# Splitting a late load, regrouping the norm work and thinning the TensorE fillers ahead of the main loop of a fused attention and feed-forward kernel

## The chip, the cores and the metric

The kernel runs on one core of a Trainium2 chip. The metric is the device time of one execution in microseconds. Engines are called as the profile calls them: PE is TensorE's matmul and PEld its weight load, DVE is VectorE, ACT is ScalarE, POOL is GpSimd and SP is SyncE; the last two mostly issue DMAs here.

## The reference, cut to what matters

Two steps are fused. The first is a cross-covariance attention over channels; the second a two-layer network with a squared ReLU. Shapes are B = 4, N = 6080, C = 256, and 2048 hidden features.

```python
qn = q / (norm(q, axis=1) + 1e-6)          # a norm for each of 256 channels, over 6080 rows
kn = k / (norm(k, axis=1) + 1e-6)
s = kn.transpose(0, 2, 1) @ qn / tau       # 256 x 256 for each batch
a = softmax(s)                             # each row divided by its sum
x = (v @ a).reshape(B * N, C)
h = maximum(x @ w_in, 0)
out = (s_moe * h * h + b_moe) @ w_out
```

## The kernel before

The attention matrix is never applied to v. For each batch the kernel forms the Gram matrix of q and k, turns it into exponentials, and multiplies these by `w_in`, which gives a folded weight `wa` of 256 x 2048. The main loop then takes v in groups of 512 rows: 16 steps of `mm1` (L761, `h_ps`) with `wa`, ReLU and square on ACT and DVE, and the second product (L932, `o_ps`). The norms and Gram matrices of batches 1 to 3 are worked in between the steps of the main loop by a table of steps. The change lies in batch 0 alone, which has to be finished before the first step of the main loop.

Batch 0 goes like this. Its 6080 rows are cut into chunks (`make_chunks`): eleven chunks of 128 partitions x 4 rows, then one of 128 x 2 and one of 96 x 2, thirteen in all, numbered 0 to 12. For each chunk k and q are loaded and cast to half precision by the DMAs of the POOL queue (`Gram.load`, L137); three of the first four loads go in fp32 through the SP and ACT queues and are cast by DVE and ACT (L145). At most eight DMAs of the POOL queue are under way: each later one waits for the landing of the one eight places before.

`Gram.mm` (L154) adds a chunk to the Gram matrix `s_ps`: 2 matmuls of 256 columns for each of its rows. `norm_ops` squares the chunk, k on ACT (L185) and q on DVE (L182) or, in odd chunks, on ACT; it folds the squares of four rows to one on DVE (two adds, L199) and adds that to the sum of chunk 0 (`into_first`, L213, held as `f`).

The last `NLATE` = 3 chunks are late ones: all their k parts are loaded before their q parts, so that k's norms can be done while q is still coming. Their squares are kept apart (`late_pool`), and `add_norms` sums them over the partitions on TensorE: for k with a matrix of ones into 256 columns (L252, one matmul for each row), for q into one column (L256, two for each row). The first late chunk's four k squares are first added to two on DVE (`half`, L229). The order of the end is written out by hand: k's squares and sums; then the chunk sum `f` (`last_sum`, the L213 of chunk 9); the inverse norms of k (`inverse`, L277: four ACT steps, Ln, Exp of a half, Ln, Exp of minus one); then for each late chunk q's squares, its matmuls and its sums, where the last chunk's sums come ahead of its matmuls; then four ACT steps for q's inverse norms, `scale` (L302, two DVE multiplications of `s_ps` by k's inverse norms), the transposes of the first v group (L469), and `first_block`. `first_block` has for each half of the channels an exponential (L308, scaled by q's inverse norm), row sums (L347) and two matmuls of 256 columns into `wa_ps` (L352); then the reciprocal `rs` (L356) and four 128-column evictions to `wa` on ACT (L329) and DVE (L331). The next blocks of `wa` are folded between the first steps of the main loop (L336).

`keep_busy` issues matmuls whose result nobody reads (fillers, L554): 512 columns of FP32R ones. `FILL` names after which chunk, counted from the end, and how many: one after each of chunks 5, 6 and 7, two after each of 8 and 9. One more stands behind the transposes of v.

The queues work in program order, which the kernel fixes with `po(...)` around each instruction.

Of the kernel before, what the change touches and what calls it, by code (L numbers as in the profile page):

```python
# [16 lines left out]
def kernel(  # L17
# [30 lines left out]
    NG = (NT + TG - 1) // TG  # L48
    NP = FT // 2
    SHIFT = 3  # L50
    NLATE = 3
    assert CH == 2 and FT == 16
    v_flat = v.rearrange("b n c -> (b n) c")

    def po(ins):

        tc.keep_in_program_order(ins)
        return ins
# [47 lines left out]
        return chunks  # L106

    whole = N // (P * JC)
    chunks_first = make_chunks([JC] * whole + [2, 2])
    chunks_later = make_chunks([JC] * (whole + 1))  # L110

    class Gram:
# [7 lines left out]
        def load(self, c, parts=(0, 1)):  # L120

            at, np_, jc = self.chunks[c]
            if 0 in parts:
                self.raw[c] = qk_pool.tile([P, 2, JC, C], FP16, tag="qk", name="qk")
            t = self.raw[c]
            for i in parts:
                src = (k, q)[i]
                rows = src[self.b, at : at + np_ * jc, :].rearrange("(p j) c -> p j c", j=jc)
                if self.b == 0 and (c, i) in DIRECT:
                    if c == i == 0:  # L130
                        for h, queue in enumerate((nc.sync, nc.scalar)):
                            ps = ts(h, P // 2)
                            queue.dma_start(out=raw32[ps, 0], in_=rows[ps])
                    else:
                        (nc.sync, nc.scalar)[i].dma_start(out=raw32[:, DIRECT.index((c, i))], in_=rows)
                else:
                    po(nc.gpsimd.dma_start(out=t[:np_, i, :jc, :], in_=rows))  # L137
            self.tiles[c] = t[:, 1], t[:, 0]

        def cast(self, c):  # L140

# [21 lines left out]
        def norm_ops(self, c):  # L163

            qc, kc = self.tiles[c]
            _, np_, jc = self.chunks[c]
            st = {}

            at_end = self.b == 0 and c >= len(self.chunks) - NLATE

            def squares(a, js):
                def f():
                    if "sq" not in st:
                        if at_end:
                            st["sq"] = late_pool.tile([P, 2, jc, C], FP16, tag=f"sq{c}", name="sq")
                        else:
                            st["sq"] = sq_pool.tile([P, 2, JC, C], FP16, tag="sq", name="sq")
                    if a == 1 and at_end and c == len(self.chunks) - 1:
                        po(nc.vector.tensor_mul(
                            st["sq"][:np_, 1, js, :], kc[:np_, js, :], kc[:np_, js, :]))  # L180
                    elif a == 0 and (self.b > 0 or at_end or c % 2 == 0):
                        po(nc.vector.tensor_mul(  # L182
                            st["sq"][:np_, 0, js, :], qc[:np_, js, :], qc[:np_, js, :]))
                    else:
                        po(nc.scalar.activation(  # L185
                            out=st["sq"][:np_, a, js, :], in_=(qc, kc)[a][:np_, js, :],
                            func=AF.Square))
                return f

            def fold(half, arrays, last):  # L190
                def f():
                    src = st["f", 2 * half] if 2 * half < jc else st["sq"]
                    if ("f", half) not in st:
                        if last:
                            t = f3_pool.tile([P, 2, 1, C], FP16, tag="f3", name="f3")
                        else:
                            t = sq_pool.tile([P, 2, half, C], FP16, tag=f"f{half}", name="f")
                        st["f", half] = t
                    po(nc.vector.tensor_add(  # L199
                        st["f", half][:np_, arrays], src[:np_, arrays, :half, :],  # L200
                        src[:np_, arrays, half : 2 * half, :]))
                    if last and c == 0:
                        self.first = st["f", half]
                    if last and c == 0:
                        for rows in self.rows:
                            rows.append((st["f", half], np_, 1))
                return f

            def into_first():

                dst, src = self.first[:np_], st["f", 1][:np_]
                if self.b == 0:
                    po(nc.vector.tensor_add(dst, dst, src))  # L213
                else:
                    po(nc.gpsimd.dma_start(out=dst, in_=src, accum_op=ALU.add))  # L215

            def unfolded(a):
                self.rows[a].append((st["sq"], np_, jc))

            ops = []  # L220
            for h in range(0, jc, 4):
                js = slice(h, min(h + 4, jc))
                ops += [squares(1, js), squares(0, js)]
            if at_end:
                def rows(a):
                    if a == 0 or jc == 2:
                        return unfolded(a)
                    half = sq_pool.tile([P, 2, 2, C], FP16, tag="f2", name="half")
                    po(nc.vector.tensor_add(half[:np_, 1], st["sq"][:np_, 1, :2], st["sq"][:np_, 1, 2:]))  # L229
                    self.rows[1].append((half, np_, 2))  # L230
                return ops + [rows]
            if jc == 8:
                ops += [fold(4, slice(0, 1), False), fold(4, slice(1, 2), False)]
            ops += [fold(2, slice(0, 2), False), fold(1, slice(0, 2), True)]
            return ops + [into_first] if c > 0 else ops
# [24 lines left out]
        def finish_ops(self):  # L260
# [3 lines left out]
            def inverse(a=None):  # L264

                n = C + CH if a is None else (CH, C)[a]

                def part(i):
                    if i == 0:
                        st["r", a] = sm_pool.tile([P, n], FP32, tag=f"r{a}", name=f"r{a}")  # L270
                        if a is None:
# [20 lines left out]
                self.add_norms(1)  # L292
                self.add_norms(0, last=True)

            def scale(halves=1):
                rk, src = st["r", 1], st.get("t", self.s_ps)
                if "t" not in st:
                    st["t"] = sm_pool.tile([P, CH, C], FP32, tag="sm_t", name="sm_t")
                for h in range(halves):
# [40 lines left out]
            def first_block(n):  # L340
# [3 lines left out]
                for j in range(CH):  # L344
# [4 lines left out]
                                            stop=(ch == CH - 1 and j == CH - 1),  # L349
                                            skip_group_check=True))  # L350
                    for m in range(CH):
                        po(nc.tensor.matmul(two[m], st["e"][:, j, ts(m, P)],  # L352
                                            w_in16[:, j, :n],
                                            start=(j == 0), stop=(j == CH - 1)))
                st["rs"] = sm_pool.tile([P, CH], FP32, tag="rs", name="rs")
                po(nc.vector.reciprocal(out=st["rs"], in_=r_ps))  # L356
                for f0 in range(0, n, P):
# [71 lines left out]
            if self.b == 0:  # L429
                blocks = [(2 * P, 2 * P), (4 * P, 2 * P), (6 * P, 2 * P), (2 * NW, NW), (3 * NW, NW)]  # L430
                folds = [fold_one(f0, n, m) for f0, n in blocks for m in range(CH)]
                return [norms(1), *inverse(1), norms(0), *inverse(0), lambda: scale(CH),
                        lambda: first_block(2 * P)] + folds

            def sums_and_halves():
# [75 lines left out]
                out=ident16, in_=ones_id, compare_op=ALU.is_equal, fill=0.0, base=0,  # L511
                pattern=[[-1, P]], channel_multiplier=1))

    for parts in ((0,), (1,)):
        for c in range(len(g0.chunks) - NLATE, len(g0.chunks)):
            g0.load(c, parts)
    NW = 512
    w_in_rows = moe_w_in.rearrange("(co p) f -> p co f", p=P)

# [26 lines left out]
    g0.start()  # L546
    NCH0 = len(g0.chunks)

    FILL = {-8: 1, -7: 1, -6: 1, -5: 2, -4: 2}

    def keep_busy(n):

        for _ in range(n):
            po(nc.tensor.matmul(h_tile("idle_ps")[:, 0, :], fill[:, :P], fill, start=True,  # L554
                                stop=True, skip_group_check=True))

    norms_k, *rest = g0.finish_ops()
    inverse_k, norms_q, inverse_q, scale_s, first_block, folds = (
# [2 lines left out]
    for c in range(NCH0 - NLATE):  # L561
        ops = g0.norm_ops(c)
        for j in range(g0.chunks[c][2]):
            g0.mm(c, j)
        keep_busy(FILL.get(c - NCH0, 0))
        if c == NCH0 - NLATE - 1:
            ops, last_sum = ops[:-1], ops[-1]
        for f in ops:
# [26 lines left out]
    keep_busy(1)  # L595
# [47 lines left out]
    def w_in_sums(i):  # L643
# [1 line left out]
        F = Dff // 2  # L645
        B = lambda k, n: w_in16[:, k, ds(n * F, F)]
        if not W:
            c0, c1, c2 = range(NCH0 - NLATE, NCH0)
            W["T1"] = late_pool.tile([P, F], FP16, tag=f"sq{c1}", name="T1w")
            W["T2"] = late_pool.tile([P, F], FP16, tag=f"sq{c2}", name="T2w")  # L650
            both = late_pool.tile([P, 2, F], FP16, tag=f"sq{c0}", name="TNw")
            W["T3"], W["N4"] = both[:, 0], both[:, 1]
# [376 lines left out]
```

## Time and profile before

| | us |
|---|---|
| median of 3 runs | 714.32 (714.3 to 714.35) |
| span of the profiled execution | 712.9 |
| time of the profiled execution beside its span | not given by the page |
| first `h_ps` matmul of the main loop (L761) | 37.84 |
| last k transfer on the chain of waits, start and length | 21.00, 9.47 |
| TensorE busy in 38 to 710 us | 671.96 of 672 |

The page counts busy time for each engine, shows the span in 40 slices, and follows the chain of work that ended last. PEclk is the clock granted to TensorE as a share of full speed. Its record begins at 16.8 us here; earlier stretches are printed as 1.00, though the 27 matmuls that start between 11 and 16.5 us take 420 ns on average, and the 20 that start between 17 and 20 us take 276 ns. Times of instructions are counted from the start of the span.

### The profile page before, as it was taken

Reading aid. Unit: us, or ns where it says so; the run is one execution under the profiler, and the core shown is the slowest. Engines: PE = TensorE matmul, PEld = TensorE weight load, DVE = VectorE, ACT = ScalarE, POOL = GpSimd, SP = SyncE. Lnnn points to the kernel's source line nnn. Section 1 sums busy time; section 2 is a strip of 40 time slices with the busy share of each in tenths; the row PEclk is TensorE's granted clock in tenths of the full one; section 3 lists DMA queues with packets and bytes.
Section 4 is the critical chain, followed back from the end, with each engine's and each line's share of the span. In section 5 each row is a group of like instructions: output and inputs, shape, how many; then the busy total and the mean of one; then the engine's idle time right before and its main releaser. Section 6 shows DMA issues by size and latency. Waiting matters only on the chain.

```text
span 712.9 us, 17531 instructions
## 1 busy us (share of the span) xinstructions
PE 692.9 (97%) x7422; PEld 502.9 (71%) x7422; DVE 635.6 (89%) x906; ACT 547.5 (77%) x598; POOL 114.1 (16%) x192
## 2 busy tenths in 40 slices
PE   3699999999999999999999999999999999999998
PEld 2456777776677777777677777777768777777777
DVE  4889999999988989998999899998998888888886
ACT  5689877787777777778877777777876777777875
POOL 4533132201202222111010222111000000000000
PEclk9999999999999999999999999999999999999999
DMA  9999999566566878465761888737323333321202
GB/s 213 207 259 168 186 164 137 114 109 122 105 136 109 133 137 144 110 92 101 156 131 50 148 134 150 129 76 96 101 65 75 94 71 75 97 61 46 83 31 75
DMA packets 87854, 83.55 MB, mean 117 GB/s; under 512 B 56368, under 2 KB 62784, under 8 KB 87776
## 3 DMA queue, kind: packets, MB, share of 16 engines
q0 software_dynamic: 27136, 44.00, 38.9%
q1 hardware_dynamic: 60128, 37.45, 21.1%
q8 instruction: 58, 0.95, 0.6%
q10 hardware_dynamic: 512, 0.98, 0.4%
q14 instruction: 20, 0.16, 0.1%
HBM read 78.91 MB, written 24.90 MB: 146 GB/s over the span
## 4 chain that ended last, share of the span: by engine, by line
PE 95%; DMA 4%; ACT 1%; issue 0%; DVE 0%; ACTq 0%; POOLq 0%
PE h_ps L761 46%; PE o_ps L932 40%; PE s_ps L154 5%; DMA qk<-in_q_dram 2%; DMA qk<-in_k_dram 1%; PE wa_ps L394 1%; PE o_ps L836 1%; PE o_ps L808 0%; PE wa_ps L336 0%; ACT r L277 0%; PE n_ps L252 0%; ACT sq L185 0%; ACT eT L308 0%; PE vT_ps L469 0%; DVE half L229 0%
## 5 line engine op out<-in xcount | busy, mean ns | idle before, releaser
L771 ACT ACTIVATE r<-h_ps 128x1024 f16<-128x1024 f32 (+1 forms) x384 | 388.5, 1013 | 144.2 <-PE h_ps L761 140.6
L761 PE MATMUL h_ps<-vT,wa 128*128 128x512 f16 (+7 forms) x1632 | 452.1, 364 | 0.5 <-ACT wa L329 0.5
L932 PEld LDWEIGHTS <-S 128*128 128x128 f16 x2944 | 198.1, 98 | 84.3
L932 PEld LDWEIGHTS <-g 128*128 128x128 f16 x2208 | 155.0, 98 | 74.0
L784 DVE TENSOR_TENSOR g<-r 128x2048 f16<-128x2048 f16 (+2 forms) x150 | 174.4, 1163 | 10.1 <-ACT r L771 9.7
L932 PE MATMUL o_ps<-T,S 128*128 128x128 f16 x2208 | 183.1, 219 | 0.0
L761 PEld LDWEIGHTS <-wa 128*128 128x128 f16 x1632 | 136.6, 98 | 19.0 <-ACT wa L329 1.0
L932 PE MATMUL o_ps<-w_out,g 128*128 128x128 f16 x1472 | 134.2, 219 | 0.0
L782 ACT ACTIVATE g<-r 128x1024 f16<-128x1024 f16 (+1 forms) x97 | 100.3, 1034 | 0.2
L789 DVE SCALAR_TENSOR_TENSOR o_sb<-o_ps,s_out,u 128x256 f32<-128x256 f32 x138 | 66.2, 480 | 36.1 <-PE o_ps L932 34.5
L154 PE MATMUL s_ps<-qk 128*128 128x256 f16 (+1 forms) x384 | 71.0, 287 | 15.6 <-ACT qk L145 11.0
L458 POOL DMA_DIRECT2D v<-in_v_dram x48 | 31.4, 662 | 239.9 <-DMA vT<-v 192.7
L215 POOL DMA_DIRECT2D f<-f x33 | 28.8, 874 | 245.9 <-DVE f L199 197.3
L789 DVE SCALAR_TENSOR_TENSOR u<-o_ps,s_out,rowconst 128x256 f32<-128x256 f32 x138 | 65.7, 476 | 0.0
L932 PE MATMUL o_ps<-w_out,S 128*128 128x128 f16 x736 | 63.5, 219 | 0.0
L932 PE MATMUL o_ps<-N,g 128*128 128x128 f16 x736 | 63.4, 219 | 0.0
L185 ACT ACTIVATE sq<-qk 128x1024 f16<-128x1024 f16 (+2 forms) x53 | 54.5, 1041 | 4.5 <-DMA qk<-in_k_dram 1.9
L861 DVE TENSOR_TENSOR S<-S,g 128x2048 f16<-128x2048 f16 (+1 forms) x47 | 56.4, 1200 | 1.2
L859 DVE TENSOR_TENSOR S<-g 128x2048 f16<-128x2048 f16 (+1 forms) x47 | 56.0, 1192 | 0.0
L863 DVE TENSOR_TENSOR S<-g 128x2048 f16<-128x2048 f16 x46 | 55.8, 1214 | 0.0
L865 DVE TENSOR_TENSOR S<-g,S 128x2048 f16<-128x2048 f16 x46 | 55.8, 1213 | 0.0
L154 PEld LDWEIGHTS <-qk 128*128 128x128 f16 (+1 forms) x384 | 33.0, 103 | 21.2 <-ACT qk L145 11.0
(103 smaller groups left out, 334.4 us busy)
## 6 DMA issues: line engine op xcount, KB each, us to landing
out_dram<-o_sb SPq DMA_DIRECT2D x43, 512.0 KB, 3.0
v<-in_v_dram POOLq DMA_DIRECT2D x47, 256.0 KB, 5.0
qk<-in_q_dram POOLq DMA_DIRECT2D x43, 256.0 KB, 7.7
qk<-in_k_dram POOLq DMA_DIRECT2D x42, 256.0 KB, 6.4
f<-f POOLq DMA_DIRECT2D x30, 128.0 KB, 3.1
vT<-v SPq DMA_TRANSPOSE x182, 3.0
w<-in_moe_w_out_dram POOLq DMA_DIRECT2D x4, 512.0 KB, 9.9
out_dram<-o_sb SPq DMA_DIRECT2D x8, 256.0 KB, 4.1
```

Of the source, the lines that this page charges most:

```text
L154: po(nc.tensor.matmul(self.s_ps[:, ch, :], qc[:np_, j, ts(ch, P)], kc[:np_, j, :], start=(c == 0 and j == 0 and ch == 0), stop=(c == len(s ...
L185: po(nc.scalar.activation(out=st["sq"][:np_, a, js, :], in_=(qc, kc)[a][:np_, js, :], func=AF.Square))
L761: po(nc.tensor.matmul(dst, wa[:, ci, ts(m, P)], src, start=(ci == 0), stop=(ci == CH - 1), skip_group_check=True))
L771: po(nc.scalar.activation(out=r16[:, :, i % 2, :n], in_=h_tiles.pop((g, i))[:, :, :n], func=AF.Relu))
L782: po(nc.scalar.activation(out=dst, in_=src, func=AF.Square))
L784: po(nc.vector.tensor_mul(dst, src, src))
L789: po(nc.vector.scalar_tensor_tensor(out=dst, in0=src, scalar=s_out, op0=ALU.mult, in1=add, op1=ALU.add))
L859: po(nc.vector.tensor_add(T[1], A21, A22))
L861: po(nc.vector.tensor_sub(T[2], T[1], A11))
L863: po(nc.vector.tensor_sub(T[3], A11, A21))
L865: po(nc.vector.tensor_sub(T[4], A12, T[2]))
L932: po(nc.tensor.matmul(st[name][:, j, :], a()[:, i, ts(j, P)], w[:, i, :], start=first, stop=last, skip_group_check=True))
```

## The change

It does the following.

- Chunks: the eleventh four-row chunk of batch 0 is treated as two chunks of two rows that share one tile. There are now fourteen chunks, of which the last four, 10 to 13, are late ones. Its k part is loaded by one DMA as before, its q part by two (`load_late`).
- q's squares of the last chunk that is not late (chunk 9) are done by DVE, not by ACT.
- The `half` add is left out: all late k squares are summed as they are, nine matmuls in place of seven. `last_sum` is issued ahead of the late k squares.
- The last chunk's q sums come behind its Gram matmuls.
- q's inverse norms: the first two steps stay on ACT; then DVE adds EPS and takes the reciprocal. The first half of `scale` is put ahead of these two, the second behind them.
- `first_block`: for each half of the channels only the first 128 columns are multiplied; the other 128 follow after both.
- Fillers: one after chunk 8 and one after chunk 9, with operands read as FP32 and not FP32R. The one behind the transposes stays.
- The four late square tiles are reused for the four weight sums of the later folds, one tile each.

```diff
-    NLATE = 3
+    NLATE = 4
...
-    chunks_first = make_chunks([JC] * whole + [2, 2])
+    chunks_first = make_chunks([JC] * (whole - 1) + [2] * 4)
+    at_late = chunks_first[-4][0]
...
+        def load_late(self, i):
+            c = len(self.chunks) - NLATE
+            if i == 0:
+                self.raw[c] = qk_pool.tile([P, 2, JC, C], FP16, tag="qk", name="qk")
+                for h in range(2):
+                    t = self.raw[c][:, :, ts(h, 2)]
+                    self.tiles[c + h] = t[:, 1], t[:, 0]
+            rows = (k, q)[i][self.b, ds(at_late, P * JC)].rearrange("(p j) c -> p j c", j=JC)
+            for js in [slice(0, JC)] if i == 0 else [ts(h, 2) for h in range(2)]:
+                po(nc.gpsimd.dma_start(out=self.raw[c][:, i, js], in_=rows[:, js]))
+            for c in range(c + 2, len(self.chunks)):
+                self.load(c, (i,))
...
-                    elif a == 0 and (self.b > 0 or at_end or c % 2 == 0):
+                    elif a == 0 and (self.b > 0 or at_end or c % 2 == 0 or c == len(self.chunks) - NLATE - 1):
...
                 def rows(a):
-                    if a == 0 or jc == 2:
-                        return unfolded(a)
-                    half = sq_pool.tile([P, 2, 2, C], FP16, tag="f2", name="half")
-                    po(nc.vector.tensor_add(half[:np_, 1], st["sq"][:np_, 1, :2], st["sq"][:np_, 1, 2:]))
-                    self.rows[1].append((half, np_, 2))
+                    return unfolded(a)
...
                 def part(i):
+                    if a == 0 and i >= 2:
+                        r = st["r", 0]
+                        if i == 2:
+                            po(nc.vector.tensor_scalar_add(out=r, in0=r, scalar1=EPS))
+                        else:
+                            po(nc.vector.reciprocal(out=r, in_=r))
...
+                        return
...
-                        po(nc.tensor.matmul(two[m], st["e"][:, j, ts(m, P)],
-                                            w_in16[:, j, :n],
-                                            start=(j == 0), stop=(j == CH - 1)))
+                        po(nc.tensor.matmul(two[m][:, :P], st["e"][:, j, ts(m, P)],
+                                            w_in16[:, j, :P], start=(j == 0),
+                                            stop=(j == CH - 1), skip_group_check=True))
+                for m in range(CH):
+                    for j in range(CH):
+                        po(nc.tensor.matmul(two[m][:, P:n], st["e"][:, j, ts(m, P)],
+                                            w_in16[:, j, P:n], start=False,
+                                            stop=(j == CH - 1), skip_group_check=True))
...
-    for parts in ((0,), (1,)):
-        for c in range(len(g0.chunks) - NLATE, len(g0.chunks)):
-            g0.load(c, parts)
+    for i in range(2):
+        g0.load_late(i)
...
-    FILL = {-8: 1, -7: 1, -6: 1, -5: 2, -4: 2}
+    FILL = {-6: 1, -5: 1}
...
-        keep_busy(FILL.get(c - NCH0, 0))
+        keep_busy(FILL.get(c - NCH0, 0), lambda t: t.bitcast(FP32))
...
+    last_sum()
     for c in late:
         k_squares, _, into_rows = ops[c]
         k_squares()
         into_rows(1)
         g0.add_norms(1)
-    last_sum()
...
         ops[c][2](0)
-        if c == NCH0 - 1:
-            norms_q()
         for j in range(g0.chunks[c][2]):
             g0.mm(c, j)
         if c < NCH0 - 1:
             g0.add_norms(0)
-    for f in (*inverse_q, scale_s):
+        else:
+            norms_q()
+    for f in (*inverse_q[:2], lambda: scale_s(0), *inverse_q[2:], lambda: scale_s(1)):
         f()
```

More of the change, by code (lines that the diff above doesn't have):

```diff
@@ L268, in part @@
                 def part(i):
+                    if a == 0 and i >= 2:
[4 more added lines that the diff above has]
+                            po(nc.vector.reciprocal(out=r, in_=r))
+                            if inv_tau != 1.0:
+                                po(nc.vector.tensor_scalar_mul(out=r, in0=r, scalar1=inv_tau))
+                        return
                     if i == 0:
@@ L293, in norms_both, with scale @@
                 self.add_norms(0, last=True)
-            def scale(halves=1):
-                rk, src = st["r", 1], st.get("t", self.s_ps)
+            def scale(halves=1, only=None):
+                rk, src = st["r", 1], st.setdefault("src", st.get("t", self.s_ps))
                 if "t" not in st:
                     st["t"] = sm_pool.tile([P, CH, C], FP32, tag="sm_t", name="sm_t")
-                for h in range(halves):
+                for h in range(halves) if only is None else (only,):
                     js = slice(h, h + 1) if halves == CH else slice(0, CH)
@@ L431, in finish_ops @@
                 folds = [fold_one(f0, n, m) for f0, n in blocks for m in range(CH)]
-                return [norms(1), *inverse(1), norms(0), *inverse(0), lambda: scale(CH),
+                return [norms(1), *inverse(1), norms(0), *inverse(0), lambda h: scale(CH, h),
                         lambda: first_block(2 * P)] + folds
@@ L547, with keep_busy @@
     NCH0 = len(g0.chunks)
-    FILL = {-8: 1, -7: 1, -6: 1, -5: 2, -4: 2}
-    def keep_busy(n):
+    FILL = {-6: 1, -5: 1}
+    def keep_busy(n, cast=lambda t: t):
         for _ in range(n):
-            po(nc.tensor.matmul(h_tile("idle_ps")[:, 0, :], fill[:, :P], fill, start=True,
-                                stop=True, skip_group_check=True))
+            po(nc.tensor.matmul(h_tile("idle_ps")[:, 0, :], cast(fill)[:, :P], cast(fill),
+                                start=True, stop=True, skip_group_check=True))
     norms_k, *rest = g0.finish_ops()
@@ L647, in w_in_sums @@
         if not W:
[L648 to L652, printed above, removed]
+            for c, name in zip(range(NCH0 - NLATE, NCH0), ("T1", "T2", "T3", "N4")):
+                W[name] = late_pool.tile([P, F], FP16, tag=f"sq{c}", name=f"{name}w")
         po([lambda: nc.vector.tensor_sub(W["T1"], B(0, 1), B(0, 0)),
```

## The prediction

> **What bounds the kernel now.** First the page: its engines and the chain that ended last.
>
> ```profile
> PE 692.9 (97%) x7422; PEld 502.9 (71%) x7422; DVE 635.6 (89%) x906; ACT 547.5 (77%) x598; POOL 114.1 (16%) x192
> ...
> PE 95%; DMA 4%; ACT 1%; issue 0%; DVE 0%; ACTq 0%; POOLq 0%
> ```
>
> TensorE is the chain, so what matters is where it is not busy. Second, the busy time in two stretches (span; PE, PEld, DVE, ACT, POOL busy; clock, DMA share, GB/s):
>
> ```profile
> 0.00:38.00 38.00, 20.91 (x146) 14.38 (x147) 24.60 (x54) 23.18 (x31) 19.90 (x38) 0.96 1.06 209
> 38.00:710.00 672.00, 671.96 (x7277) 488.48 (x7275) 610.65 (x853) 524.28 (x568) 94.24 (x154) 1.00 0.59 112
> ```
>
> From 38 us on TensorE is never free: 671.96 of 672. Every edit lies ahead of that, so the change is worth exactly the shift of the first `h_ps` matmul (L761, 37.84 us); nothing later can be shortened. DMA is saturated all through the first stretch (share 1.06). Third, the chain around the turn from loading to computing:
>
> ```profile
> 21.00 9.47 DMA qk<-in_k_dram
> ...
> 30.49 1.06 ACT sq L185
> ...
> 31.58 0.43 DVE half L229
> ...
> 32.06 0.95 PE n_ps L252 x7
> ...
> 33.03 0.48 ACT r L277
> ...
> 34.53 0.60 ACT r L277 x2
> ...
> 35.95 0.52 ACT eT L308
> ...
> 37.42 0.38 ACT wa L329
> ...
> 37.84 0.60 PE h_ps L761 x2
> ```
>
> Last k lands, squares, folds, k's norm sums, four ScalarE steps for 1/|k|, four for 1/|q|, exponentials, first block. Fourth, TensorE in order of time there, which the chain hides:
>
> ```profile
> 32.73 0.27 PE L252 MATMUL n_ps<-f,ones 128*128 128x256 f16 x1
> 32.91 1.05 PE L154 MATMUL s_ps<-qk 128*128 128x256 f16 x8
> 33.79 0.19 PE L256 MATMUL n_ps<-ones,f 128*128 128x1 f16 x2
> ...
> 34.48 0.34 PE L256 MATMUL n_ps<-ones,sq 128*128 128x1 f16 x8
> 34.68 0.60 PE L154 MATMUL s_ps<-qk 96*128 96x256 f16 x4
> ```
>
> It is packed from 32.06 to 35.28. The last q sums end at 34.82, just as ScalarE could take 1/|q| (34.86): two chains tie. Fifth, the clock, in stretches of 3.41 us between its changes:
>
> ```profile
> 20.21:23.62 3.41, 1.63 (x12) 0.93 (x10) 3.27 (x7) 1.72 (x3) 1.08 (x3) 1.00 1.11 208
> 23.62:27.04 3.42, 1.56 (x12) 1.15 (x13) 3.18 (x8) 2.65 (x3) 1.59 (x4) 1.00 1.13 211
> 27.04:30.45 3.41, 3.38 (x16) 2.04 (x14) 2.15 (x5) 2.11 (x2) 1.75 (x3) 0.50 1.13 205
> ```
>
> After two thinly used stretches the granted clock is 0.50 for one stretch, which was full (3.38), and then 1.00 again. Before it costs nothing: TensorE had finished its fillers at 31.4 and waited for VectorE until 32.06.
>
> **The base.** The page gives the profiled execution's span, 712.9; no other time of it is shown. The sum is made in that span, and its difference goes onto the median of the runs, 714.32, which lies 1.4 above.
>
> **Part by part.** Prices on TensorE: a 256-column matmul starts every 0.109 (two sums take 0.38, one 0.27), a one-column sum every 0.025 (eight 0.34, two 0.19).
>
> *Loads.* q's 512 KB chunk becomes two transfers: one more POOL issue (0.53; POOL is idle before most issues), and v and w_in are issued one landing later, about 1.2. They landed 5.8 to 7 after issue behind a saturated queue, so only smaller packets count: the two short k transfers, 448 KB, took 1.15, while 512 KB takes 1.25, so 448 at that rate 1.09. That is 0.06 per such pair; all later landings move by +0.06. v then lands at 35.40, w_in's second piece at 37.97; its reader L336 started at 38.29. Hidden; if that slack is gone, 0.06.
>
> *q squares of chunk 9 on VectorE.* They start at the landing, 29.26, where VectorE sat idle 1.08, and take 0.69. The folds then start at 30.08 instead of 30.37, and, put ahead of the late k squares, the last L213 ends at 31.71 instead of 32.68. The `half` add (0.42) goes too. k's sums now wait for ScalarE: three 512-element squares from 30.49, 0.52 apart (two squares took 1.58, and 1024 elements one by one 1.06), end at 32.14.
>
> *k's sums.* Nine instead of seven, but the last five alone follow 32.18: the ninth starts at 32.62 and ends at 32.89. 1/|k| starts at 32.93, not 33.03, so ScalarE is free for 1/|q| at 34.76 (0.10 earlier). This supposes TensorE free at 31.2.
>
> *q's sums and the order.* After k's sums TensorE has 16 matmuls (1.74) and 18 column sums (0.45), from 32.73: 34.92, and 0.14 to drain, 35.06. q's halves have landed by then at each step (about 32.3, 32.9, 33.6, 34.06), so the split of the transfer does not matter; TensorE does. Before, the last column sums went ahead of the last four matmuls (0.44); now they come behind them. So Ln for q starts at 35.10, not 34.86: +0.24. `s_ps` is finished earlier (about 34.97, not 35.28), but its reader, the first `scale` half, is not the last thing needed.
>
> *1/|q| ends on VectorE.* Before, Ln to first exponential took 1.09. Now Ln 0.29, Exp 0.20, 0.03 across, an add, a reciprocal. The trace has no such add; nearest are a 128x1 TENSOR_SCALAR of 0.146 (L670) and the 128x2 reciprocal of 0.171 (L356), with the 0.059 memset as the low end for each. With 0.06 and 0.05 for the two hand-overs that is 0.95 (0.75 to 1.1, 0.95 taken since two rows of the same kinds give it). First exponential: 36.05 against 35.95, **+0.10** (-0.10 to +0.25). The add waits for ScalarE; behind it on VectorE stand the second `scale` half (0.42, ready at about 36.45, when the second exponential, 0.42 after the first, wants it) and the vT copy (0.68, wanted at 37.84 and before the reciprocal L356): hidden, up to 0.05 otherwise.
>
> *First block 128 wide.* The first halves are ready about 0.1 sooner, but `wa` (37.42) also waits for `rs`, which ends at 37.33 and does not move. Gain 0 (at most 0.05). The four later half matmuls, 4 x 0.057 (the eight 128-wide transposes take 0.62), lie in the 0.48 that TensorE waits for ScalarE; uncovered they would cost 0.23.
>
> *Fillers.* Seven FP32R fillers of 0.215 go; two in FP32 come, after chunks 8 and 9. What FP32 costs stands in the rowconst matmul:
>
> ```profile
> L610 PE MATMUL rc_ps<-acc,ones x2: 379/379/379, 62.0 to 62.2; 128*128 128x256 f32 x2
> ```
>
> One 256-wide FP32 product is two matmuls 0.216 apart, so 512 columns take 0.86, and 1.7 at half clock, plus about 0.15 per exposed weight load (the two fillers at 28.07 and 28.65 stood 0.57 apart, not 0.43). At chunks 5 to 7 nothing fills the gaps: the thin stretches have 0.2 less work each, so the clock should fall at 27.04 again, or sooner. Then: chunk 8's matmuls until 28.2, its filler until 30.1, chunk 9's eight (two at 0.213, six at 0.109) until 31.2, its filler until 32.2, and the nine k sums run back to back, 0.98, to 33.18 instead of 32.73: **+0.45**. It is carried whole, since TensorE is packed from there to the q sums. If the clock stays full the filler ends at 31.2 and this is 0.
>
> The page "TensorE: Matmul & The Clock Gate" of the Trainium skill (Why this matters for your kernels) asks only that TensorE not idle for more than about 3 us between bursts; the longest such wait here is under 1.8, so by it the clock would stay full. The trace's 0.50 from 27.04 says otherwise, and I go by the trace. By the rule the sum would be +0.10, by the row +0.55.
>
> **Sum.** 0.10 + 0.45 = +0.55, less a few hundredths where ScalarE's squares cover part of it: 714.85.
>
> **Rivals.**
> *Full clock* (0.2): +0.10, 714.4. For it: fillers four times as long. Against: they come after the thin stretches.
> *A real gain* (0.1): the add and reciprocal at their low ends and the q sums not TensorE-bound, -0.2, 714.1. It cannot pass -0.32: w_in's second piece lands at 37.97, and L336 stood at 38.29.
> *The clock comes back too late* (0.2), the slower side: changes lie 3.41 apart, and recovery needs a full stretch. With this kernel a full stretch can begin only at 26.76, so recovery falls between 30.2 and 33.6, as the grid lies. At 33.6: chunk 9 cold until 31.8, its filler until 33.6, k's sums until 34.6, +1.9 +0.10: 716.3. Between, about 0.45 per us: from a recovery at 32.4 the loss passes 1.43. Against it: three runs within 0.05 us, where a cold stretch elsewhere would have shown in the old kernel too (up to about 0.9).
> The forecast itself has 0.5.
>
> **The numbers.** 0.2% is 1.43 us, about what a measurement of this kernel can tell from no change. Faster by that is beyond the w_in bound: 0.02. Slower by that is the upper half of the late-clock case and a little for stacked small losses: 0.13. The rest, 0.85. The range runs from near the real gain, 714.1, to 715.8, the middle of the late clock.
>
> **What would show it.** Right: the first exponential at 36.2 to 36.6, L213 done near 31.7, q's Ln after the last `s_ps` matmul has started, clock 0.50 until about 30.4, k sums back to back after a long filler, `h_ps` at 38.2 to 38.5. Wrong: q's Ln at 34.9 or earlier; a full clock throughout; `wa` starting earlier relative to the exponentials; a half clock beyond 32; TensorE idle after 38.5.

## The result, and the profile after

The changed kernel takes 715.17 us (median of 21 runs, 714.82 to 716.78); the kernel before took 714.41 beside it (21 runs, 714.13 to 714.73). The ratio is 1.0015 (95% interval 1.0009 to 1.0021): a loss of 0.76 us, inside the 0.2% that the prediction called no change, and 0.32 above its 714.85. It is a right answer with two mis-sized terms in it.

The page's time of the profiled execution is 714.96, its span 713.3. First the stretches after, cut at the first `h_ps` matmul (span; PE, PEld, DVE, ACT, POOL busy; clock, DMA share, GB/s):

```profile
38.25:710.00 671.75, 671.75 (x7274) 488.40 (x7275) 610.81 (x853) 524.73 (x568) 94.73 (x155) 1.00 0.60 112
```

TensorE is again never free behind that matmul, so its shift, 37.84 to 38.25, is the whole loss of this execution. The chain of waits of the kernel after shows what sets it now:

```profile
20.81 9.47 DMA qk<-in_k_dram
...
30.56 6.61 DMA w_in<-in_moe_w_in_dram
...
37.21 0.28 PE wa_ps L372 x2
...
37.83 0.38 ACT wa L349
...
38.25 0.61 PE h_ps L782 x2
```

Squares, k's sums and both inverse norms are off the chain; a load of `w_in` stands in their place. Next TensorE in order of time, kernel after; the bracket is the idle time before a group and what ended it (groups run into each other, and their ends overlap):

```profile
30.89 1.02 PE L578 MATMUL idle_ps<-fill 128*128 128x512 f32 x2
31.75 1.04 PE L263 MATMUL n_ps<-sq,ones 128*128 128x256 f16 x8
32.62 0.27 PE L263 MATMUL n_ps<-f,ones 128*128 128x256 f16 x1
...
34.40 0.60 PE L169 MATMUL s_ps<-qk 96*128 96x256 f16 x4
...
37.21 0.28 PE L372 MATMUL wa_ps<-w_in,eT 128*128 128x128 f16 x2 [0.40 <-DMA w_in<-in_moe_w_in_dram]
```

The nine k sums run back to back behind the second filler, with no wait between; the ninth starts at 32.62. The first product of the folded block waits 0.40 for the first piece of `w_in`, which lands at 37.17 (35.98 in the kernel before). Then ACT, and below it DVE, in order of time, kernel after:

```profile
32.93 0.47 ACT L297 ACTIVATE r<-n_ps,tiny 128x256 f32<-128x256 f32 x1 [0.96 <-PE n_ps L263]
...
35.11 0.26 ACT L297 ACTIVATE r<-n_ps,tiny 128x2 f32<-128x2 f32 x1 [0.26 <-PE n_ps L267]
...
36.04 0.91 ACT L328 ACTIVATE eT<-sm_t,r 128x256 f16<-128x256 f32 x2 [0.44 <-DVE r L285]
```

```profile
35.64 0.17 DVE L283 TENSOR_SCALAR r<-r 128x2 f32<-128x2 f32 x1
35.84 0.17 DVE L285 RECIPROCAL r<-r 128x2 f32<-128x2 f32 x1
```

1/|k| starts at 32.93, q's Ln at 35.11, the first exponential at 36.04. Last, the clock in its own stretches, kernel after:

```profile
23.23:26.65 3.42, 1.97 (x9) 1.12 (x10) 3.18 (x7) 2.85 (x3) 1.59 (x3) 0.50 1.11 207
26.65:30.06 3.41, 3.41 (x11) 1.72 (x12) 3.13 (x7) 1.06 (x1) 1.59 (x3) 0.50 1.13 208
30.06:33.47 3.41, 3.41 (x32) 2.58 (x31) 2.61 (x7) 2.17 (x5) 2.91 (x5) 1.00 1.24 203
```

Two half-clock stretches instead of one, but they end at 30.06.

**Why that load is late.** The DMA records hold, beside the loads, transfers of instructions; in the window 35.0 to 36.0 the kernel after has one (queue and kind: packets, MB, share of 16 engines):

```profile
q8 instruction: 1, 0.02, 6.1%
```

It is 16 KB and lies at 35.03 for 0.98 us; in the kernel before the first one of this size lies at 35.89. Of the sixteen shares of `w_in`'s first piece fifteen have landed by 35.80 and one at 37.17, 1.4 later; 16 KB at a sixteenth of the 204 GB/s that the loads run at would be 1.3. In the kernel before the same happened to the second piece (37.91 against 36.61 for the other shares), which is read later. The records do not name the engine of a packet, so that the late share and the transfer stood in one engine's queue is inferred. Something stands behind it in all the profiles of this document: in thirteen of the fourteen the first load whose last share lands 0.59 us or more behind its fifteenth is one that begins to land after the first 16 KB transfer has started (in the fourteenth, e1, the largest gap there is 0.43), and ahead of the transfer no gap is over 0.39. The theory to test: in the changed kernel the transfer comes earlier and holds back a load that is waited for, and its place goes with the instructions ahead of it. It is not that the changed kernel gives TensorE more of them: ahead of the transposes of v the trace has 255 matmuls and weight loads after and 257 before.

### The profile page after: what moved, and what is told of

It is laid out like the page before. It is cut to its first block, busy times and chain, and to the rows that moved or that the text cites. A ratio compares the mean times of both kernels' runs of the same rounds, so it can differ in the third digit from the quotient of the medians.

```text
span 713.3 us, 17539 instructions
## 1 busy us (share of the span) xinstructions
PE 693.7 (97%) x7425; PEld 503.2 (71%) x7425; DVE 636.6 (89%) x909; ACT 546.4 (77%) x596; POOL 115.0 (16%) x193
## 4 chain that ended last, share of the span: by engine, by line
PE 94%; DMA 5%; issue 0%; POOL 0%; ACT 0%; DVE 0%; POOLq 0%
PE h_ps L782 46%; PE o_ps L953 40%; PE s_ps L169 4%; DMA qk<-in_k_dram 4%; PE wa_ps L419 1%; PE o_ps L857 1%; DMA w_in<-in_moe_w_in_dram 1%; PE o_ps L829 0%; PE wa_ps L356 0%; POOL qk L138 0%; PE vT_ps L494 0%; PE rc_ps L634 0%; PE wa_ps L372 0%; ACT wa L349 0%; DVE o_sb L835 0%
```

## Experiments

The runs came in three groups, e, c1 to c4 and c5 to c8, each with its own runs of the kernel before: medians 714.38 (31 runs, up to 714.91), 714.50 (33, up to 716.11) and 714.34 (33, up to 715.85). In the eight kernels whose names begin with c, v's transposes by DMA (SP's queue, all after 38 us) are plain copies, so that v is not transposed there. All durations below come from one profiled execution of each kernel.

| kernel | first 16 KB instruction transfer | exponential minus 1/&#124;k&#124; start | `h_ps` minus exponential | median, fastest | minus before | above 716 |
|---|---|---|---|---|---|---|
| before | 35.89 | 2.92 | 1.89 | 714.41, 714.13 | | 0 of 21 |
| after | 35.03 | 3.11 | 2.21 | 715.17, 714.82 | +0.76 | 5 of 21 |
| e1 before again | 36.14 | 2.92 | 1.89 | 714.42, 714.36 | +0.04 | 0 of 11 |
| e2 after again | 35.22 | 3.11 | 2.47 | 715.12, 714.85 | +0.74 | 2 of 11 |
| e3 after, old fillers | 34.54 | 3.11 | 2.76 | 715.44, 714.74 | +1.06 | 4 of 9 |
| e4 before, new fillers | 35.72 | 2.90 | 1.89 | 714.41, 714.19 | +0.03 | 0 of 11 |
| c1 before | 35.69 | 2.91 | 1.89 | 714.50, 714.26 | 0.00 | 0 of 11 |
| c2 after | 35.42 | 3.11 | 1.89 | 714.91, 714.80 | +0.41 | 3 of 11 |
| c3 before, ten more | 32.69 | 4.12 | 1.90 | 715.62, 715.22 | +1.12 | 1 of 11 |
| c4 after, twelve fewer | 35.97 | 3.11 | 1.89 | 714.91, 714.48 | +0.41 | 1 of 11 |
| c5 after, no fillers | 35.49 | 3.11 | 1.88 | 714.62, 714.32 | +0.28 | 0 of 11 |
| c6 after, old q end | 35.33 | 3.03 | 2.52 | 715.18, 714.85 | +0.84 | 3 of 11 |
| c7 after, wide Gram | 36.16 | 3.32 | 1.89 | 714.48, 714.22 | +0.14 | 1 of 12 |
| c8 after, three fillers behind v | 35.27 | 3.11 | 2.14 | 715.09, 714.57 | +0.75 | 2 of 11 |

**Both kernels again.**

> The kernel before, unchanged, to see a second profiled execution. Theory A (what delays the changed kernel in its profile is a 16 KB instruction transfer that runs at 35.0 us instead of 35.9 and holds back one sixteenth of w_in's first piece): here w_in's first piece lands near 36.0 again and the first h_ps matmul starts near 37.85. Rival B (the instruction transfer's place is chance, different in each execution of the same kernel): it may fall anywhere between 34.9 and 36, and w_in's first piece lands at 36.0 or near 37.2. Time 714.1 to 714.7 with either. Theory C (clock): the half-clock stretches begin and end at other places than 27.04 and 30.45, since nothing ties their grid to the start of the program; if they lie at the same place within 0.3 us, the grid is tied.

> The changed kernel, unchanged, a second profiled execution. Theory A: the instruction transfer starts near 35.0 again, w_in's first piece lands near 37.2, TensorE waits 0.4 us for it in the first block. Rival B: in this execution it may land near 35.8 and the wait be gone. Theory C: runs spread from 714.8 to 716.8, depending on where the half-clock stretch ends; if this profile's stretch ends after 31 us, its k sums start later than the 31.75 of the first profile by as much as the fillers are stretched.

Both medians came back: 714.42 (ratio 1.0001, 0.9992 to 1.0010) and 715.12 (1.0014, 1.0005 to 1.0022). In e2 the first piece of `w_in` is late again (37.26, the other shares 35.77) and TensorE waits 0.7 for it. Its profiled execution, 716.57, is one of the long ones, and its stretches tell what makes a long one (columns as above):

```profile
34.67:38.08 3.41, 2.00 (x27) 1.34 (x24) 1.91 (x7) 1.53 (x5) 1.78 (x4) 1.00 1.32 201
38.08:41.49 3.41, 3.15 (x11) 1.69 (x12) 1.02 (x3) 1.31 (x4) 2.35 (x4) 0.50 1.19 233
```

After a stretch with TensorE busy for only 2.00 of 3.41, the first stretch of the main loop runs at half clock: 1.6 us lost where nothing hides it.

**The fillers, each set in the other kernel.**

```diff
 e3, in the kernel after:
-    FILL = {-6: 1, -5: 1}                          # read as FP32
+    FILL = {-9: 1, -8: 1, -7: 1, -6: 2, -5: 2}     # read as FP32R
 e4, in the kernel before:
-    FILL = {-8: 1, -7: 1, -6: 1, -5: 2, -4: 2}     # read as FP32R
+    FILL = {-5: 1, -4: 1}                          # read as FP32
```

> The changed kernel with the old fillers: one FP32R filler after each of chunks 5, 6 and 7 and two after each of 8 and 9. Theory C (the two FP32 fillers make the long tail of the changed kernel, because TensorE is still behind when the clock comes back late): the runs above 715.8 disappear and the spread shrinks to about 0.6 us; the median falls by 0.1 to 0.4, to about 714.8 to 715.0, since the 0.1 of q's inverse norms and the 0.3 of w_in remain. Rival D (the fillers do not matter, the spread comes from DMA): spread and median as with the changed kernel, 715.2. The filler instructions change TensorE's instruction count by +6, so the instruction transfer may start earlier by up to 0.2 us; w_in's first piece then still lands near 37.2.

> The kernel before with the new fillers alone: one FP32 filler after each of chunks 8 and 9, none elsewhere. Theory C: the long tail appears here too, runs from 714.3 up to about 716, median up by 0.1 to 0.5. Rival D: no tail, 714.4 within 0.1. My prediction's step (+0.45 from the fillers in the usual case) expects a median near 714.85.

The new fillers cost the old kernel nothing: 714.41 (1.0002, 0.9993 to 1.0010), with the half clock over by 27.81. The old fillers do not mend the new kernel: 715.44 (1.0022, 1.0013 to 1.0032). In e3's profile the granted clock is 1.00 throughout, yet `h_ps` starts at 38.56. Its transfer is the earliest of the after kind so far, 34.54, and hits v; the waits of TensorE from 28 us on (total, times, longest):

```profile
PE vT_ps L494 <- DMA v<-in_v_dram: 1.8, 1, 1.8
```

So neither the clock nor the fillers' work explains the loss; which load is hit goes with the transfer's place.

**Moving the transfer: more instructions in the kernel before, fewer in the kernel after.** c1 and c2 are the bases.

```diff
 c3, in c1, behind the fillers of the sixth-last chunk:
+        for _ in range(10):
+            po(nc.tensor.matmul(idle[:, 0, :1], ones16, ones16[:, 0:1], ...))
 c4, in c2:
-        for j in range(g0.chunks[c][2]):
+        for j in range({1: 4, 2: 2}.get(c, 0), g0.chunks[c][2]):
             g0.mm(c, j)
 c7, in c2, chunks 1 to 3: one matmul of 512 columns for two of 256
+            if c in (1, 2, 3):
+                po(nc.tensor.matmul(<all of s_ps>, qc[:, j, :P], <two rows of kc>, ...))
+                continue
             g0.mm(c, j)
```

> The kernel before, with the crossbar transposes of v (SP's queue, from the third group on, all after 38 us) replaced by plain copies of the same bytes; the transposition is left out. It is the base for the runs below. TensorE sets the time from 38 us on, so every theory gives 714.4 within 0.2 and the same first 38 us as the kernel before: h_ps at 37.8 to 37.9, instruction transfer at 35.7 to 36.2.

> The changed kernel with the same copies for the crossbar transposes. Every theory gives the changed kernel's 715.1 within 0.2, its tail above 716 in some runs, the instruction transfer at 34.5 to 35.3 and a wait of TensorE for w_in's first piece or for v.

> The kernel before with copies for the crossbar transposes, and with ten one-column FP16 matmuls (20 TensorE records) added after the sixth-last chunk, where TensorE waits for loads. Theory A (the 16 KB instruction transfer comes earlier and holds back a share of w_in's first piece or of v): the transfer, at 35.89 in the kernel before, starts 0.6 to 1.2 us earlier, at 34.7 to 35.3; the load it hits lands at 36.5 to 37.3 instead of 35.4 to 35.9; the first h_ps matmul moves from 37.84 to 38.1 to 38.5, and the median by +0.3 to +0.9 over the base with copies, with single runs above 716. Rival B (the loss lies in the changed order of sums, squares and block width): this kernel has the old order, so its time is that of its base within 0.15 and no run is above 715.2.

> The changed kernel with copies for the crossbar transposes, and without twelve of the early Gram matmuls (all of chunk 1, half of chunk 2; 24 TensorE records; that part of q k^T is left out). Theory A: the instruction transfer starts about 1.2 us later, at 36.0 to 36.5, w_in's first piece lands at 35.7 to 36.0 with all its shares, TensorE does not wait for it, h_ps starts at 37.8 to 38.0, and the median is 714.3 to 714.6 with no run above 715.3. Rival B: the order is that of the changed kernel, so its 715.1 and its tail up to 716.6 stay.

> The changed kernel with copies for the crossbar transposes, and with the 24 Gram matmuls of chunks 1 to 3 of 256 columns replaced by 12 of 512 columns (same TensorE time, 24 records fewer; those three chunks' part of q k^T is left out, other products stand in its place). It takes instructions away without making TensorE idler. Theory A: the transfer starts at 35.8 to 36.3, w_in's first piece is whole at 35.6 to 36.0, TensorE doesn't wait for it, h_ps at 37.8 to 38.0; fastest run 714.4 to 714.6, median 714.4 to 714.75. Rival B: fastest run 714.8, median 715.1. Theory C (clock): the median lies between, and what is above 716 has one more half-clock stretch.

The copies change nothing in c1 (0.9999, 0.9990 to 1.0008); c2 is 714.91 (1.0013, 1.0003 to 1.0023). Its profiled execution does not show the expected wait: the transfer lies at 35.42, `w_in`'s first piece is whole at 36.24, and `h_ps` minus exponential is 1.89. There the last k load landed late, at 30.72 against 30.27 in c1, and all that follows moved with it to 38.21. e1's profiled execution, of the kernel before, had the same (1/|k| at 33.50, 715.03), so this is no part of the change. The wait for `w_in` is thus not in every execution of the changed kernel.

c3 tests the theory directly. Ten one-column matmuls, a few hundredths of a microsecond each, placed where TensorE waits anyway, cost the old kernel 1.12 us by the medians (1.0014, 1.0005 to 1.0022). The transfer moved further than expected, to 32.69, and hit a q load: fifteen shares by 33.31, the last at 34.71. The chain of waits of c3:

```profile
25.52 9.20 DMA qk<-in_q_dram
...
34.74 0.77 DVE sq L182 x2
...
36.93 0.52 ACT eT L308
...
38.83 0.60 PE h_ps L767 x2
```

The first exponential is 1.19 later than in c1 (35.74), which is the loss; 1/|k| starts at 32.81, as in c1 (32.83), so the ten matmuls did not delay the work ahead of it. Why 20 more records (a record is a matmul or a weight load) move the transfer by 3 us, when TensorE starts 61 records in that time in c3 and 86 in c1, was not settled: the place is not a fixed count of the records in the trace (274 ran ahead of it in the kernel before, 254 after, 210 in c3). Within the changed kernel, though, it moves with their number. Counted from the landing of the last k load, the transfer starts after 4.34 us with six records more (e3), 4.70 to 4.96 with the changed kernel's own number (after, e2, c2, c6, c8), 5.22 with eight fewer (c5), and 5.74 and 5.73 with 24 fewer (c4, c7). The kernel before stands at 5.20 to 5.42 (before, e1, c1), so what brings the changed kernel's transfer forward is its order or instructions that the trace does not count; which of them stays open.

c7 is the counterpart: the changed kernel, TensorE no idler, 24 records fewer. The median falls to 714.48 (1.0001, 0.9992 to 1.0010), the fastest run from 714.80 to 714.22. With the transfer at 36.16 the first piece of `w_in` is whole at 35.95; that profile is of a very long run (below), in which TensorE itself is late, so for the fast runs the load on time is inferred from their times. The 3.32 in the table is an add of 0.39 on DVE in place of 0.18. What is left over the kernel before is 0.14, inside the interval and near the +0.10 of the prediction's step on 1/|q|.

c4 takes as many records away by leaving matmuls out. Its fastest run reached 714.48, but the median stayed at 714.91 (1.0007, 0.9998 to 1.0016). The transfer (35.97, expected at 36.0 to 36.5) and `w_in` (whole at 35.76) are about as expected; the chain of waits shows another cause:

```profile
28.41 1.71 PE idle_ps L579 x2
30.11 1.21 PE s_ps L169 x8
31.32 0.86 PE idle_ps L579 x2
32.18 0.99 PE n_ps L263 x9
```

Here is the prediction's filler step: the half clock lasts to 30.67, a filler takes 1.71, and k's nine sums run back to back until 33.17, where it put them (33.18). Whether its clock recovers late because of the twelve matmuls that it lacks was not tried.

c7's profiled execution is its one very long run, 717.91, and carries the same further (stretches as above):

```profile
29.30:32.72 3.42, 3.42 (x12) 1.76 (x11) 2.97 (x6) 1.67 (x3) 2.54 (x4) 0.50 1.21 198
32.72:36.13 3.41, 3.41 (x41) 2.78 (x40) 1.27 (x3) 1.72 (x4) 3.10 (x6) 1.00 1.27 199
36.13:39.55 3.42, 1.99 (x29) 1.33 (x26) 2.41 (x8) 1.91 (x7) 2.57 (x4) 1.00 1.25 207
39.55:42.96 3.41, 3.41 (x13) 1.86 (x14) 0.97 (x3) 1.31 (x3) 1.34 (x3) 0.50 1.10 318
```

The clock recovers at 32.72 and k's sums end at 34.28; then a stretch with TensorE busy 1.99 of 3.42 is followed by a half clock at the main loop's start, as in e2. `h_ps` starts at 39.53.

**Undoing the fillers, undoing the q end.**

```diff
 c5, in c2:
-    FILL = {-6: 1, -5: 1}
+    FILL = {}
 c6, in c2: four ACT steps for 1/|q|, and
+        if c == NCH0 - 1:
+            norms_q()
         for j in range(g0.chunks[c][2]):
             g0.mm(c, j)
         if c < NCH0 - 1:
             g0.add_norms(0)
-        else:
-            norms_q()
-    for f in (*inverse_q[:2], lambda: scale_s(0), *inverse_q[2:], lambda: scale_s(1)):
+    for f in (*inverse_q, lambda: scale_s(0), lambda: scale_s(1)):
```

> The changed kernel with copies for the crossbar transposes, without its two FP32 fillers (eight TensorE records fewer). Theory A (the place of the instruction transfer costs the time): the transfer starts at 35.4 to 35.9, the wait for w_in's first piece shrinks or goes, the fastest runs reach 714.4 to 714.6 as with twelve Gram matmuls fewer, median 714.4 to 715.0. Rival B (order of sums, squares and block width): no run below 714.8, as in the changed kernel. Theory C (the clock decides, as in the profile with twelve Gram matmuls fewer): without fillers TensorE is used less at 28 to 32, so a half clock beyond 31 us, k's sums ending after 33.2 and more runs above 715.3.

> The changed kernel with copies for the crossbar transposes and with q's old end: its last norm sums ahead of the last four Gram matmuls, all four steps of 1/|q| on ScalarE, both scalings after them. By the prediction's step (+0.10 from that edit) the first exponential comes 0.05 to 0.15 earlier relative to the end of k's sums (3.14 after it instead of 3.23 in the changed kernel's profile, where k's last sum ended at about 32.81). Theory A: the number of TensorE instructions is the same, the instruction transfer stays where it is, w_in's first piece or v still lands late, so the fastest run stays at 714.8 within 0.1 and the median within 0.2 of the changed kernel's. Rival B (the q end is where the time went): the median falls to 714.5 or lower.

Without the two fillers the transfer lies at 35.49 (35.42 in c2), `w_in`'s first piece is whole at 35.79, and the median to 714.62 (1.0004, 0.9995 to 1.0013), with no run above 715.88. Two things may have gained this, the transfer's place and the fillers' own time, and since c2's profile shows no wait for `w_in` either, c5 does not tell them apart. What was expected of the clock came in part: c5's profiled execution (714.50) has half clock until 32.12, but with no filler in TensorE's way k's sums are not late. The chain of waits of c5:

```profile
35.91 0.92 ACT eT L328 x2
...
37.79 0.61 PE h_ps L783 x2
```

The old q end leaves the time at 715.18 (1.0016, 1.0007 to 1.0024). It does bring the first exponential forward, by 0.08 (3.03 against 3.11 behind the start of 1/|k|; 0.05 to 0.15 was expected), but the load is what is waited for. Waits of TensorE in c6:

```profile
PE wa_ps L372 <- DMA w_in<-in_moe_w_in_dram: 0.7, 1, 0.7
```

**More work where TensorE waits.**

```diff
 c8, in c2:
     transpose_v(0)
-    keep_busy(1)
+    keep_busy(3)
```

> The changed kernel with copies for the crossbar transposes, with three instead of one of the FP32R fillers between v's transposes and the first block (0.43 us more work where TensorE waits for the exponentials). Theory C (the runs above 716 come from a half clock that falls on the main loop's start because TensorE is thinly used at 35 to 38): no run above 716, the fastest stays at 714.8 to 715.0, median 714.9 to 715.1. If the tail has another cause: two to four of eleven runs above 716 as before. If the fillers come in the way of the first block: all runs later by 0.1 to 0.4.

The forecast of no run above 716 failed (716.05 and 716.43 of 11), and the median stayed at 715.09 (1.0011, 1.0002 to 1.0020). The edit did what it was to do in the profile: the thinnest 3.41 us around 35 to 38 hold 2.59 us of TensorE work, as in the kernel before, and not 2.01 as in the kernel after. No run of c8 shows a mean clock below 0.995, while the runs above 716.4 of the kernel after, of c2 and of c6 show 0.992 or 0.993 (three half-clock stretches take 5.1 of 713 us, which is 0.993). But the mean counts stretches and does not place them: e3's two longest runs, 717.20 and 717.30, have 0.997. What made c8's two long runs is open; a late recovery as in c7 fits, and no profile of such a run was taken.

No kernel here beats the kernel before. The best of the after kind that leaves no work of the Gram matrix out, c5, is 0.28 slower by the medians, inside its interval.

## Why the prediction was right, and where it was wrong

- **The bound** held: TensorE is never free behind the first `h_ps` matmul, and the shift of that matmul, 0.41, is the change of span (712.9 to 713.3).
- **Squares, k's sums, q's order, q's end** were right in size, and their places on the time axis, given here as forecast without the fillers' 0.45, were met by luck. The last L213 add (L228 now) ended at 31.51 (31.71 predicted), the three late k squares at 31.97 (32.14), 1/|k| started at 32.93 (32.93), q's Ln at 35.11 (35.10); add and reciprocal took 0.17 each (0.146 and 0.171 from the nearest rows). The first exponential came at 36.04 (36.05; with the fillers 36.2 to 36.6 was named, and that sign failed). But the last k load landed at 30.28 in this execution, 0.19 ahead of the 30.47 that the prediction starts from, and 1/|k| lost about as much behind the fillers (two points below). Counted from that landing, 1/|k| starts after 2.49 where no filler stands in the way (e2, e3, c2, c6), against 2.56 to 2.57 in the five profiles of the old order (before, e1, e4, c1, c3): k gains 0.07, not 0.10. q's end costs 0.19 (3.11 against 2.92), not 0.20. Together +0.12 for +0.10.
- **First block 128 wide**, gain 0: right. `h_ps` minus exponential is 1.88 to 1.90 in every kernel, 256 or 128 wide, in which neither v nor `w_in`'s first piece is late.
- **Fillers, +0.45: the mechanism was right, the size was that of one execution.** In the profile after they cost about 0.16: from the landing of the last k load to 1/|k| it takes 2.65, and the k sums stand behind a filler. In e2, where the half clock ended earlier, the eight sums start sooner and are spread over 1.64 by their waits for the squares, and the ninth starts at 32.45 after the same landing (30.27):

```profile
30.97 1.64 PE L263 MATMUL n_ps<-sq,ones 128*128 128x256 f16 x8
32.45 0.27 PE L263 MATMUL n_ps<-f,ones 128*128 128x256 f16 x1
```

  The cost follows the end of the half clock:

| profile | half clock ends | from landing of the last k load to 1/&#124;k&#124; |
|---|---|---|
| e2 | 27.84 | 2.49 |
| after | 30.06 | 2.65 |
| c8 | 30.41 | 2.81 |
| c4 | 30.66 | 2.97 |
| c7 | 32.72 | 3.89 |
| c5, no fillers | 32.12 | 2.53 |

  The step took that end from one trace, 30.45; c8, at 30.41, pays 0.32. From after to c7 the cost grows by 0.47 for each us, close to the 0.45 that the prediction's late rival uses. But the place moves between executions of one kernel: the half clock lasted from 21.53 to 28.36 in e1, from 27.04 to 30.45 in the first trace. In e4 the fillers cost 0.03 by the medians, and its profile has the half clock over by 27.81. So it was a term for some executions, not a fixed part of the sum.
- **Loads, hidden, +0.06: wrong.** The step carried the landings of before over by a shift of +0.06 and checked the second piece of `w_in`, which indeed was the late one in that trace. It did not ask why that piece's last share landed 1.3 behind the others. The cause moved by 0.86 us and the lateness went to the first piece, which is read earlier. This is the +0.32 of the profiled execution (2.21 against 1.89), and 0.58 and 0.63 in e2 and c6.
- **The sum** came out near by exchange: the predicted +0.55 was 0.10 and 0.45 for the fillers; the profiled execution has 0.12, 0.16 for the fillers and 0.32 for the load, less the 0.19 by which its k load happened to land earlier, which makes the 0.41. So `h_ps`, at 38.25, fell into the 38.2 to 38.5 that the prediction named by a load that it had called hidden. That landing belongs to the execution: in e1 and c1, both of the old order, it is at 30.94 and 30.27. The median's +0.76 holds executions with a longer wait: c6's profile, of a run at its median of 715.18, has 0.63.
- **The rivals.** Full clock (+0.10) had the granted clock back before the k sums, and by the median of c7, +0.14, would have been near with the load on time. "The clock comes back too late", 716.3, is where the long runs lie; c7's profile shows its mechanism, with a recovery at 32.72. The other half of it was not foreseen: the half clock at the main loop's start in e2 and c7. The prediction looked for idle time of TensorE behind 38.5, not for a slow TensorE. Its "recovery needs a full stretch" was too strict: in e2 a half-clock stretch with 2.84 of 3.41 was followed by full clock.
- **The page "TensorE: Matmul & The Clock Gate"** of the Trainium skill (Why this matters for your kernels), cited in the prediction with its advice of no idle gap over about 3 us, did not foretell the clock in either place. In e2 the stretch before the fall holds no wait longer than 0.7 us, in c7 none longer than 1.0, and the clock was halved. TensorE's busy time in the stretch ahead does not foretell it either: it was 2.00 and 1.99 of 3.41 there, but e3 kept the full clock all through with less, as did c4 (1.55) and the kernel before (1.63) for a stretch each. Two stretches of e3 one after the other:

```profile
22.32:25.73 3.41, 1.73 (x12) 1.02 (x10) 3.20 (x7) 2.58 (x3) 1.52 (x4) 1.00 1.12 210
25.73:29.14 3.41, 1.62 (x11) 1.12 (x12) 3.17 (x8) 1.65 (x2) 1.31 (x3) 1.00 1.13 210
```

  What brings the fall stays open.

## What to carry to other kernels

Where the loads are the bound, look at the landing of every share of a load that is waited for, not at the median share: one late share of sixteen is a sign of something else in the queues, and it can move to another load with an edit to the instructions ahead. A filler is not free even where its engine is idle: it adds instructions, and in an execution where the clock is low it takes twice its time and stands ahead of real work. When two small terms are worked out from one trace, ask of each whether its place on the time axis is set by the program or by that one execution, and compare executions from a common event, such as a landing, not from the start.

## What the runs showed of the hardware that was not expected

The kernel's instructions share the DMA engines with its data: 58 transfers on queue 8 in the run, 16 KB each, 0.97 or 0.98 us where it mattered. Behind the first of them one share of a load came 1.2 to 1.5 us after the other fifteen in ten of the fourteen profiles, and moving it with ten matmuls of one column cost 1.12 us. The granted clock is decided in stretches of 3.41 us whose place differs between executions of the same kernel; two stretches just ahead of the packed main loop with TensorE busy 2.00 and 1.99 of 3.41 were each followed by one at half clock, though stretches with less were followed by full clock elsewhere. The way back is more regular: in the fourteen profiles, up to 50 us, every half-clock stretch with 2.82 us or more of TensorE work was followed by full clock (15), and every one with 2.62 or less by another at half clock (12).
